# One visit instead of two for the scan outputs of blocks four to six, fewer and wider dummies at the start, and new planner settings

## The chip, the core and the metric

The kernel runs on one core of a Trainium2 chip, alone. The metric is device time of one execution in microseconds (us). A core has five engines with a queue of instructions each: PE (TensorE, the matmuls, with PEld for its weight loads), DVE (VectorE), ACT (ScalarE), POOL (GpSimd) and SP (SyncE, which here issues nearly all DMAs). [...]

## The reference, cut to what matters

A decaying linear attention runs over 768 positions in chunks; its output `y` is the input of a gated feed-forward network. There are 4 batches, 8 heads, head size 32 and state size 16; the network is 256 wide with 1536 hidden units.

```python
L = np.exp(cum[:, :, :, None] - cum[:, :, None, :]) * causal      # decays inside a chunk
M = np.einsum('bhin,bhjn->bhij', Cc, Bc) * L                      # scores
y_intra = np.einsum('bhij,bhjd->bhid', M, xc)
y_inter = np.einsum('bhin,bhnd->bhid', Cc, state) * decay_to_i[:, :, :, None]
y[:, :, sl] = y_intra + y_inter
state = decay_full[:, :, None, None] * state + np.sum(Bx, axis=2)
...
g, val = x @ w_gate, x @ w_val            # x: y of all heads side by side
return (g * (1.0 / (1.0 + np.exp(-g))) * val) @ w_out
```

## The kernel before, in words

The positions are cut into six blocks of 128 (`k` = 0 to 5 in the code, blocks one to six in the text), and each block into two pieces of 64. For each block PE does two short stretches of small fp32 matmuls. The first, `sums` and `scores`, makes the state sums (tiles `st`) and the scores (tiles `S`) in one go. The second, `outputs`, makes `y`: for each batch `values` adds scores times `x` (tiles 64 rows by 32 columns of the array, reading `L` and `xb`), then `carried` adds the earlier state (32 by 64, reading `bc` and `T`). Each such matmul of the program runs as two passes on the chip, and each pass is two instructions, a weight load and a matmul. So `outputs` of two batches is 64 passes of `values` and 32 of `carried`, 192 instructions.

Between these stretches stands the network. A hidden group `f` (twelve of 128 units) has gate and value banks `gv`, and its part of the output product goes to the banks `po`. These are matmuls of 512 columns in fp32r, three for each product (high times high, low times high, high times low), two instructions each; only the first eight groups of block one use whole fp32 (tiles `xf`, two passes per matmul). Part of block four, and blocks five and six as a pair, use a scheme with seven products in place of eight on sums of quarters (tiles `hx`, `hy`, `hz`; `px`, `py`, `pz`, `pr`; in the closing product `ox`, `oy`, `oz`, `or`). The high and low parts of the weights are made on ACT and DVE (`w_high`, `w_low`), and the whole weights are written back to DRAM (tiles `uncut`) for the sums that the scheme needs.

The order on every engine comes from a planner. Each operation is given an engine, a cost, a due time (its rank), what it needs, and the buffers that it takes and gives back; the planner then plays the program through, choosing the earliest due of the operations that are ready. `LEAD` says how long before a block's first hidden group its scan work is due; `LATER`, `MAKE`, `MAKE_STEP`, `AHEAD`, `URGENT`, `OUT_MAKE`, `OUT_STEP`, `BEHIND`, `AFTER`, `EARLY`, `SUM_LAG` and `SCAN_ALL` set due times and order of the preparing work on ACT and DVE, of the fetches and of the closing product, and `LATE` says which weight load the block loads of block three wait behind. In blocks two to six the output passes are planned as two visits of two batches, with a pause between them that no engine spends:

```python
add("PE", 1.52, do(outputs, k, (0, 1)), z + 11, need, ..., gives=("y", k, 0), kind="f", ...)
add("~", 2.6, lambda: None, z, [("y", k, 0)], gives=("pause", k))
add("PE", 1.52, do(outputs, k, (2, 3)), z + 11, [("pause", k)], ..., gives=("y", k), kind="f")
```

All users of `y` (`x_high`, `x_low`, `half_keep`, `x_keep`) wait for the second visit. Before the first real matmuls PE runs dummies (tile `rest`, function `idle`), 28 of 100 columns each.

Of the kernel before, what the change touches and what calls it, by code (L numbers as in the profile page):

```python
# [17 lines left out]
BATCH, H, S, D, N = 4, 8, 768, 32, 16  # L18
# [10 lines left out]
NF = DFF // P  # L29
# [14 lines left out]
class Plan:  # L44
# [26 lines left out]
    def add(self, engine, cost, run, rank, needs=(), takes=(), uses=(), gives=None, kind=None, lag=0.0, rows=1.0, slack=0.0):  # L71
        engines = [(engine, cost)] if cost is not None else engine
        self.ops.append(Op(engines, run, rank, needs, takes, uses, gives, kind, lag, rows, slack))
# [139 lines left out]
def scan_moe_kernel(ctx: ExitStack, tc, rows, decays, bc, xb, wgv, wo, cst, out):  # L213
# [847 lines left out]
    def do(f, *a):  # L1061
        return lambda *e: f(*a, *e)
# [6 lines left out]
    add = plan.add  # L1069
# [30 lines left out]
    for n, ranks in enumerate(IDLE):  # L1100
        for i, r in enumerate(ranks):
            need = [("idle", n, i - 1)] if i else [("idle", n - 1, len(IDLE[n - 1]) - 1)] if n else []
            if n:
                need = need + [(("S", 0, BATCH - 1), ("vals", 0), ("y", 0))[n - 1]]
            takes = [] if i or n else [("at", "rest")]
# [32 lines left out]
    for k in range(NB):  # L1138
        r = due(k)
        SLACK = min(k / 2, 1.0)  # L1140
        z = -5 if not k else r + LEAD[k]
        L, E, BC, XB, CZ, TT = ("L", k), ("E", k), ("bc", k), ("xb", k), ("Cz", k), ("T", k)
# [16 lines left out]
        if not k:  # L1159
# [3 lines left out]
            for b in range(BATCH + 1):  # L1163
                for i in range(2 if b < BATCH else 1):
# [7 lines left out]
                    need = [t, ("decays", 0), "dj"] + ([("scan0", b - last_one)] if i else []) + ([("M", 0, NP - 2)] if b == BATCH else [])  # L1172
# [16 lines left out]
        y = [("y", k, i) for i in range(2 * K)]  # L1189
        for bs in [(b,) for b in range(BATCH)] if not k else [range(BATCH)]:  # L1190
# [4 lines left out]
            if k in JOINED:  # L1195
# [3 lines left out]
                need = [("bt", k, BATCH - 1), ("Cz", k)]  # L1199
# [11 lines left out]
        for q in range(0 if k else 1, len(st)):  # L1211
            need = [*before, ("E", k), ("ap", k, q)] + ([] if k or q > 1 else [("ap", k, 0), ("round", 2)])
            add("DVE", 0.785, do(step, k, q), z + (8 if k else 25) + q, need, uses=[] + ([("T", k - 1)] if k and not q else []), gives=("step", k, q))
            before = [("step", k, q)]
        uses = [L, E, XB, BC, *y, TT]
# [3 lines left out]
        for g in range(0 if k else 2):  # L1219
            need = [("M", 0, p) for p in (2 * g, 2 * g + 1)]  # L1220
            add("PE", 0.45, do(values, 0, range(BATCH), (g,)), -1.4 + 0.1 * g, need, takes=[("mm", y[2 * q + g]) for q in range(K)], uses=[L, XB, *y], gives=("vals", g), kind="f")
        if k:
            need = [*(("M", k, p) for p in range(NP)), ("ce", k), *steps]
            add("PE", 1.52, do(outputs, k, (0, 1)), z + 11, need, takes=[("at", i) for i in y], uses=y, gives=("y", k, 0), kind="f", slack=min(k - 0.5, 2.5))
            add("~", 2.6, lambda: None, z, [("y", k, 0)], gives=("pause", k))
            add("PE", 1.52, do(outputs, k, (2, 3)), z + 11, [("pause", k)], uses=[L, *uses], gives=("y", k), kind="f")
        for b in range(0 if k else BATCH):
            add("PE", 0.135, do(carried, 0, b), -1, [("vals", 0), ("vals", 1), ("ce", 0), *steps], uses=uses, gives=("y", 0) if b == BATCH - 1 else ("y", 0, b), kind="f")
        done = [("y", k)]
# [71 lines left out]
    for r in range(NF // 2):  # L1301
        at = OUT_MAKE + OUT_STEP * r
        i = NF + r
        u = [("sg", ("out", r, n)) for n in range(2)]
        add("DVE", 0.6, do(whole_again, r), at, [("wl", i), ("wh", i), ("round", NW - 1), MIXED_AFTER, *prior], takes=u, gives=("ws", i, -1))
        uses = [key for _, key in u]
# [6 lines left out]
    for k in (*HALVED, PAIR):  # L1313
        for f in user(k):
            other = in_raw(f) if k == PAIR else f in LOOSE.get(k, ())
            need = [("spared", f), *behind, *(["new_t1", "new_t2"] if other and k == PAIR else [("xtl", k, 1)] if other else [])]
# [20 lines left out]
    for f in range(NF):  # L1337
# [27 lines left out]
        for b in range(2):  # L1365
            home, need = stay_home(f // 2, f"{f % 2 + 1}{b + 1}")
# [3 lines left out]
    for r in range(R):  # L1370
        at = due(PAIR, 2 * r + 1) + SUM_LAG
        pr = [("pr", PAIR + b, 2 * r + o) for b in range(2) for o in range(2)]
        for n, (t, *_) in enumerate((("t1",), ("t3",), ("t2",), ("t4",))):
            home, need = stay_home(r, t) if t != "t3" else ([], [])
            add("DVE", 0.6, do(stay_sum, r, n), at + n * 0.1, [*(pr if not n else [("ksum", r, n - 1)]), *need], takes=home, gives=("ksum", r, n))

    at = due(PAIR) + 60.0
# [23 lines left out]
    for j, (n, r, h) in enumerate(steps):  # L1401
# [5 lines left out]
        uses = [tile_of[b]]  # L1407
# [109 lines left out]

CST = W + 2 + 2 * D + 2 * P
NA = NB * K * BATCH * H // P
WARM = 28, 100  # L1520
IDLE = [-9.0] * WARM[0], [-1.45] * 4, [-1.35] * 2, [1000.0] * 3
LATER = 2.4
ST_ONE, ST_MM, JOINED = (), (1, 2, 3, 4), (1, 2, 3, 4)
LEAD = {1: -27.4, 2: -41.8, 3: -59.2, 4: -69.7, 5: -56.2}
PAIR_LAG, MIXED, RAW = 5.0, 4, 4
MIXED_AFTER = ("y", 1)
HALVED = {3: 4}
HALF_AT = "z"
MAKE, MAKE_STEP = 114.1, 3.3
LOOSE = {3: (3, 5, 7)}  # L1530
AHEAD, URGENT = 13.9, 58.5


def in_raw(f):
    return f >= MIXED and f % 2 == 0


OUT_MAKE, OUT_STEP = 181.0, 1.4
OUT_RAW = 1, 3, 5
BEHIND, AFTER = 0.9, 0  # L1540
MORE = 3
EARLY, SUM_LAG = 7.7, 8.0
STAYS = "11", "12", "21", "22", "t1", "t2", "t4"
SPARE = ("L", 0), ("E", 0), ("bc", 0), ("xb", 0), ("Cz", 0), ("T", 0), ("T", 1), ("dj", 0), ("dn", 0), ("w", 0)
MADE = (
# [15 lines left out]
    return f >= HALVED.get(k, NF)  # L1561


SCAN_ALL = 18.0
WHOLE = 8
LATE = {2: NF + 2}
GATE, HASTE = dict(bc=0, aj=0, xb=0, an=1), 7
HELD = {1: ("M", 0, 0), 2: ("M", 0, 1), 3: ("M", 0, 3)}

# [51 lines left out]
```

## Time and profile before

| | |
|---|---|
| runs of the kernel before, us | 336.28, 338.09, 338.64 (median 338.09) |
| profiled execution, us | 336.26 |
| its span, first to last instruction, us | 334.5 |
| PE busy | 328.5 us, 98% |
| DVE busy | 290.1 us, 87% |
| ACT busy | 192.6 us, 58% |
| DMA moved | 57.68 MB, mean 172 GB/s |

The profiled execution is 1.76 us longer than its span. The chain is the view that follows the last instruction back to what released it. A timeline row gives the start, the time until its last instruction's end, the instruction with its tiles and shapes, how many of a kind stand in a row (x), and in brackets how long the engine was idle before and who ended that; "issue" there means that the profile shows nothing that was waited for.

### The profile page before, as it was taken

Reading aid. Unit: us, or ns where it says so; the run is one execution under the profiler, and the core shown is the slowest. Engines: PE = TensorE matmul, PEld = TensorE weight load, DVE = VectorE, ACT = ScalarE, POOL = GpSimd, SP = SyncE. Lnnn points to the kernel's source line nnn. Section 1 sums busy time; section 2 is a strip of 40 time slices with the busy share of each in tenths; the row PEclk is TensorE's granted clock in tenths of the full one; section 3 lists DMA queues with packets and bytes.
Section 4 is the critical chain, followed back from the end, with each engine's and each line's share of the span. In section 5 each row is a group of like instructions: output and inputs, shape, how many; then the busy total and the mean of one; then the engine's idle time right before and its main releaser. Section 6 shows DMA issues by size and latency. Waiting matters only on the chain.

```text
span 334.5 us, 7903 instructions
## 1 busy us (share of the span) xinstructions
PE 328.5 (98%) x3196; PEld 259.6 (78%) x3199; DVE 290.1 (87%) x556; ACT 192.6 (58%) x360; POOL 4.2 (1%) x11
## 2 busy tenths in 40 slices
PE   8899999999999999999999999999999999999995
PEld 7634567888887888888888889998788888888784
DVE  5999999977988996998999955986768999989994
ACT  3686998365564663444464445543755556554982
POOL 1300000000000000000000000000000000000000
PEclk9999999999999999999999999999999999999999
DMA  6699569992011996466994399442047511330011
GB/s 246 223 306 335 209 201 341 292 211 75 17 33 38 248 375 212 175 222 213 270 386 174 125 315 186 136 151 105 2 126 252 189 58 72 123 125 0 3 64 63
DMA packets 21277, 57.68 MB, mean 172 GB/s; under 512 B 2296, under 2 KB 3320, under 8 KB 21240
## 3 DMA queue, kind: packets, MB, share of 16 engines
q1 hardware_dynamic: 20808, 56.94, 53.5%
q8 instruction: 25, 0.41, 0.5%
q10 hardware_dynamic: 432, 0.23, 0.2%
q14 instruction: 12, 0.10, 0.1%
HBM read 41.23 MB, written 15.93 MB: 171 GB/s over the span
## 4 chain that ended last, share of the span: by engine, by line
PE 97%; DMA 1%; issue 1%; DVE 0%; ACT 0%; DVEq 0%
PE gv L202 35%; PE po L202 20%; PE py L202 7%; PE y L202 5%; PE px L202 5%; PE oy L202 4%; PE hy L202 3%; PE pz L202 2%; PE pr L202 2%; PE ox L202 2%; PE S L202 2%; PE hz L202 2%; PE hx L202 2%; PE a L202 2%; PE st L202 1%; PE or L202 1%
## 5 line engine op out<-in xcount | busy, mean ns | idle before, releaser
L202 ACT CAST hh<-sg 128x512 fp32r<-128x512 f32 (+1 forms) x54 | 29.3, 556 | 32.2 <-PE po L202 24.5
L202 DVE TENSOR_TENSOR hl<-sg,hh 128x512 fp32r<-128x512 f32 (+1 forms) x56 | 32.8, 608 | 8.6 <-ACT hh L202 8.3
L202 ACT ACTIVATE sg<-gv 128x512 f32<-128x512 f32 x40 | 23.9, 599 | 26.8 <-PE gv L202 24.7
L202 DVE TENSOR_TENSOR sg<-gv,sg 128x512 f32<-128x512 f32 x40 | 27.2, 684 | 4.5 <-PE gv L202 4.5
L202 DVE TENSOR_TENSOR_SCAN L<-L,dj 128x520 f32<-128x520 f32 x20 | 24.1, 1228 | 0.0
L202 DVE TENSOR_TENSOR ws<-ws 128x128 f32<-128x128 f32 (+1 forms) x60 | 20.0, 364 | 1.9 <-ACT ws L202 1.6
L202 DVE TENSOR_TENSOR L<-S,L 128x512 f32<-128x512 f32 x24 | 15.6, 683 | 3.5 <-PE S L202 3.5
L202 ACT ACTIVATE sg<-px 128x512 f32<-128x512 f32 x12 | 7.2, 599 | 15.9 <-PE px L202 15.9
L202 PE MATMUL py<-xht,ws 128*128 128x512 f32 x48 | 15.3, 400 | 0.0
L202 DVE TENSOR_TENSOR hlt<-stt,hht 128x512 fp32r<-128x512 f32 x18 | 11.7, 686 | 0.9 <-ACT hht L202 0.7
L202 PEld LDWEIGHTS y<-L,xb 64*32 64x32 f32 x768 | 8.5, 105 | 4.5 <-issue 4.1
L202 ACT ACTIVATE sg<-pz 128x512 f32<-128x512 f32 x12 | 7.2, 599 | 7.2 <-PE pz L202 7.2
L202 PE MATMUL y<-L,xb 64*32 64x64 f32 x768 | 10.6, 224 | 0.4 <-issue 0.4
L202 ACT CAST ws<-ws 128x512 fp32r<-128x512 f32 x10 | 6.2, 622 | 8.2 <-DVE ws L202 6.7
L202 ACT ACTIVATE Cz<-bc,cs 128x512 f32<-128x512 f32 x12 | 8.0, 716 | 4.7 <-DMA bc<-in_bc 4.7
L202 PEld LDWEIGHTS py<-xht,ws 128*128 128x128 f32 x48 | 8.6, 188 | 2.7 <-DVE pz L202 1.2
L202 DVE TENSOR_TENSOR ps<-py,ps 128x512 f32<-128x512 f32 x12 | 8.3, 689 | 2.6 <-PE py L202 2.6
L202 ACT CAST hht<-stt 128x512 fp32r<-128x512 f32 x17 | 9.8, 620 | 0.7 <-DVE stt L202 0.6
L202 DVE TENSOR_TENSOR pz<-py,ps 128x512 f32<-128x512 f32 x12 | 8.3, 695 | 1.3 <-PE py L202 1.0
L202 PE MATMUL py<-xlt,ws 128*128 128x512 f32 x24 | 9.3, 389 | 0.0
L202 PE MATMUL y<-bc,T 32*64 32x64 f32 x352 | 7.6, 223 | 0.2 <-issue 0.2
L202 ACT COPY py<-px 128x512 f32<-128x512 f32 x12 | 6.9, 574 | 1.3
(792 smaller groups left out, 974.2 us busy)
## 6 DMA issues: line engine op xcount, KB each, us to landing
ws<-keep SPq DMA_DIRECT2D x20, 512.0 KB, 4.3
keep<-ws SPq DMA_DIRECT2D x12, 512.0 KB, 7.3
L<-clipped SPq DMA_DIRECT2D x10, 520.0 KB, 9.3
xb<-in_xb SPq DMA_DIRECT2D x6, 768.0 KB, 10.3
bc<-in_bc SPq DMA_DIRECT2D x6, 512.0 KB, 8.9
ws<-uncut SPq DMA_DIRECT2D x12, 256.0 KB, 3.1
wos_k<-keep SPq DMA_DIRECT2D x6, 512.0 KB, 3.6
out<-ob SPq DMA_DIRECT2D x8, 256.0 KB, 4.1
```

Source lines behind the costliest of these rows:

```text
L202: ins = getattr(self.engine, name)(*a, **k)
```

## The change: what it does

For blocks four to six (`MERGED = 3, 4, 5`) the two visits become one: `outputs` of all four batches, first 128 passes of `values`, then 64 of `carried`, 192 passes or 384 instructions; the pause goes. Blocks two and three keep two visits. The dummies become 11 of 256 columns. Fourteen further settings of the planner get other numbers.

```diff
         if k:
             need = [*(("M", k, p) for p in range(NP)), ("ce", k), *steps]
-            add("PE", 1.52, do(outputs, k, (0, 1)), z + 11, need, takes=[("at", i) for i in y], uses=y, gives=("y", k, 0), kind="f", slack=min(k - 0.5, 2.5))
-            add("~", 2.6, lambda: None, z, [("y", k, 0)], gives=("pause", k))
-            add("PE", 1.52, do(outputs, k, (2, 3)), z + 11, [("pause", k)], uses=[L, *uses], gives=("y", k), kind="f")
+            takes = [("at", i) for i in y]
+            if k in MERGED:
+                add("PE", 2.64, do(outputs, k, range(BATCH)), z + 11, need, takes=takes, uses=[L, *uses], gives=("y", k), kind="f", slack=min(k - 0.5, 2.5))
+            else:
...
-WARM = 28, 100
+WARM = 11, 256
...
-LATER = 2.4
+LATER = 3.3
...
-LEAD = {1: -27.4, 2: -41.8, 3: -59.2, 4: -69.7, 5: -56.2}
+LEAD = {1: -31.9, 2: -52.2, 3: -70.6, 4: -74.9, 5: -46.5}
...
-MAKE, MAKE_STEP = 114.1, 3.3
+MAKE, MAKE_STEP = 122.9, 4.8
...
-AHEAD, URGENT = 13.9, 58.5
+AHEAD, URGENT = 9.0, 41.6
...
-OUT_MAKE, OUT_STEP = 181.0, 1.4
+OUT_MAKE, OUT_STEP = 174.5, 2.3
...
-BEHIND, AFTER = 0.9, 0
+BEHIND, AFTER = 0.7, 2
...
-EARLY, SUM_LAG = 7.7, 8.0
+EARLY, SUM_LAG = 0.3, 11.7
...
-SCAN_ALL = 18.0
+SCAN_ALL = 21.3
+MERGED = 3, 4, 5
...
-LATE = {2: NF + 2}
+LATE = {2: NF}
```

On PE, block four's outputs before, the first visit's end, what stands between, and the second visit's beginning (`y` are the four output banks, `xb`, `L`, `bc` and `T` the block's inputs; the rows left out are more passes of the same kinds):

```order
L202 MATMUL y_3_1941<-bc_1512,T_1489 64x64
L202 MATMUL gv_5_1_1999<-xh_920,wg5h 128x512 x2
L202 MATMUL gv_5_1_1999<-xh_920,wg5l 128x512 x2
L202 MATMUL gv_5_1_1999<-xl_921,wg5h 128x512 x2
L202 MATMUL gv_6_0_2009<-xh_920,wg6h 128x512 x2
...
L202 MATMUL gv_6_1_2020<-xl_921,wg6h 128x512 x2
L202 MATMUL y_0_1938<-L_1487,xb_1485 32x64
```

On PE, the same block's outputs now, with what stands ahead, at the seam of `values` and `carried`, and behind:

```order
L202 MATMUL po_1_0_1557<-hh_11_1734,wo5l 128x512
L202 MATMUL gv_0_1_1791<-xh_914,wg0h 128x512 x2
L202 MATMUL gv_0_1_1791<-xh_914,wg0l 128x512 x2
L202 MATMUL gv_0_1_1791<-xl_915,wg0h 128x512 x2
L202 MATMUL y_0_1804<-L_1448,xb_1446 32x64
...
L202 MATMUL y_3_1807<-L_1448,xb_1446 32x64
L202 MATMUL y_0_1804<-bc_1472,T_850 64x64
...
L202 MATMUL y_3_1807<-bc_1472,T_1450 64x64
L202 MATMUL gv_1_0_1918<-xh_914,wg1h 128x512 x2
```

The 18 matmuls of 512 columns that separated the visits have gone elsewhere. Before, the visits stood within hidden group five and behind group six of block three's network; the one visit now stands behind its group zero.

On SP, the DMA issues from the load `wo0r` on, before (`uncut` is a write of 256 KB, `wo..r` a load of 512 KB):

```order
L202 DMA wo0r<-in_wo 128x1024
L202 DMA uncut<-wg8w 128x512
L202 DMA uncut<-wg0w 128x512
L202 DMA uncut<-wg1w 128x512
L202 DMA uncut<-wg9w 128x512
L202 DMA wo1r<-in_wo 128x1024
L202 DMA uncut<-wg2w 128x512
L202 DMA uncut<-wg3w 128x512
L202 DMA uncut<-wg4w 128x512
```

On SP, the same place now:

```order
L202 DMA wo0r<-in_wo 128x1024
L202 DMA uncut<-wg8w 128x512
L202 DMA uncut<-wg0w 128x512
L202 DMA uncut<-wg1w 128x512
L202 DMA uncut<-wg2w 128x512
L202 DMA uncut<-wg3w 128x512
L202 DMA uncut<-wg4w 128x512
L202 DMA uncut<-wg5w 128x512
L202 DMA wo1r<-in_wo 128x1024
L202 DMA uncut<-wg9w 128x512
```

Seven writes now stand ahead of the load `wo1r`, where there were four, and the write of group nine stands behind it.

The change moves everything on PE against a grid of 256 instructions. Counted in the built programs from 0 (an fp32 matmul is four instructions, an fp32r one two, a wait that stands alone one), PE has 6456 instructions before and 6418 now, and the counts 192 + 256 j lie here:

| count | before | now |
|---|---|---|
| 448 | instruction 84 of block one's first `values` | instruction 118 of the same |
| 704 | first matmul of group zero's second bank (`gv`, whole fp32) | first matmul of group two's second bank |
| 1216 | 101 of block two's first output visit | 136 of it |
| 1472 | 126 of block two's second visit | 175 of it |
| 2752 | in a `po` stretch | 28 of block four's `st` and `S` |
| 3008 | 83 of the `S` part of block four | in `po`, 27 behind block four's `S` |
| 3264 | 76 of block four's first visit | 221 of its only visit |
| 3520 | 103 of block four's second visit | in `gv` |
| 4288 | 149 of block five's first visit | 205 of its only visit |
| 5312 | 98 of block six's first visit | 177 of its only visit |

Between block two's two visits stood 18 matmuls of 512 columns (group nine and half of ten); now there are 12 (group nine).

## Rows read from the trace of the kernel before

**Rows 1.** The page: busy time of the engines, instruction queue, chain that ended last.
```profile
PE 328.5 (98%) x3196; PEld 259.6 (78%) x3199; DVE 290.1 (87%) x556; ACT 192.6 (58%) x360; POOL 4.2 (1%) x11
...
q8 instruction: 25, 0.41, 0.5%
...
PE 97%; DMA 1%; issue 1%; DVE 0%; ACT 0%; DVEq 0%
```

**Rows 2.** Waits of PE in the whole span: total us, times, longest.
```profile
PE gv L202 <- PE gv L202: 0.6, 1, 0.6
PE y L202 <- issue: 0.6, 2, 0.4
```

**Rows 3.** Timeline of PE at block 4's two output visits: start, us, instruction.
```profile
147.53 0.62 PE L202 MATMUL gv<-xh,wg5l 128*128 128x512 f32 x2
147.98 0.61 PE L202 MATMUL gv<-xl,wg5h 128*128 128x512 f32 x2
148.53 0.86 PE L202 MATMUL y<-L,xb 64*32 64x64 f32 x64
149.32 0.69 PE L202 MATMUL y<-bc,T 32*64 32x64 f32 x32
149.94 0.72 PE L202 MATMUL gv<-xh,wg5h 128*128 128x512 f32 x2
150.50 0.63 PE L202 MATMUL gv<-xh,wg5l 128*128 128x512 f32 x2
...
154.26 0.86 PE L202 MATMUL y<-L,xb 64*32 64x64 f32 x64
```

**Rows 4.** The page, two groups (decay scans, output passes): count, busy us, mean ns.
```profile
L202 DVE TENSOR_TENSOR_SCAN L<-L,dj 128x520 f32<-128x520 f32 x20 | 24.1, 1228 | 0.0
...
L202 PE MATMUL y<-L,xb 64*32 64x64 f32 x768 | 10.6, 224 | 0.4 <-issue 0.4
```

**Rows 5.** Timeline of PE, start of the program.
```profile
0.82 2.49 PE L202 MATMUL rest<-const-bfloat16-1.0 128*128 128x100 bf16 x28 [0.82 <-PEq L1610]
3.43 4.88 PE L202 MATMUL a<-rows 128*128 128x260 f32 x16
...
12.67 0.42 PE L202 MATMUL y<-L,xb 64*32 64x64 f32 x21 [0.39 <-issue]
...
18.23 1.88 PE L202 MATMUL gv<-xf,wg0w 128*128 128x512 f32 x4 [0.61 <-PE gv L202]
19.94 3.60 PE L202 MATMUL gv<-xf,wg1w 128*128 128x512 f32 x8
```

**Rows 6.** Windows from 0: PE and PEld instructions begun (x) up to three waits.
```profile
0.00:12.40 12.40, 11.19 (x220) 8.75 (x221) 9.01 (x19) 4.73 (x9) 4.19 (x11) 1.00 0.61 209
0.00:18.10 18.10, 15.82 (x344) 11.46 (x348) 14.35 (x31) 8.78 (x17) 4.19 (x11) 1.00 0.72 247
0.00:55.60 55.60, 53.14 (x722) 31.74 (x725) 51.30 (x102) 42.77 (x80) 4.19 (x11) 1.00 0.80 264
```

**Rows 7.** Timeline of PE, the two output visits of block 2.
```profile
48.95 0.86 PE L202 MATMUL y<-L,xb 64*32 64x64 f32 x64
...
54.69 0.86 PE L202 MATMUL y<-L,xb 64*32 64x64 f32 x64
55.72 0.69 PE L202 MATMUL y<-bc,T 32*64 32x64 f32 x32 [0.17 <-issue]
```

**Rows 8.** Windows: last three columns are PEclk, DMA share, GB/s.
```profile
12.00:16.00 4.00, 3.29 (x148) 2.26 (x136) 3.64 (x9) 3.35 (x10) 0.00 (x0) 1.00 0.90 298
...
130.00:134.00 4.00, 4.00 (x138) 3.15 (x137) 0.91 (x3) 2.31 (x6) 0.00 (x0) 1.00 0.44 119
```

**Rows 9.** Timeline of PE, a visit of state sums and scores (block 4).
```profile
131.40 0.86 PE L202 MATMUL st<-xb 64*32 64x64 f32 x64
...
133.33 0.72 PE L202 MATMUL gv<-xh,wg0h 128*128 128x512 f32 x2
```

**Rows 10.** Timeline of DVE: the rounding that frees the second weight group.
```profile
18.58 0.68 DVE L202 CUSTOM_DVE_ANT_0 wg1w<-wg1r,wg1w 128x1024 uint16<-128x1024 uint16 x1
```

More of the change, by code (lines that the diff above doesn't have):

```diff
@@ L1223, in scan_moe_kernel @@
             need = [*(("M", k, p) for p in range(NP)), ("ce", k), *steps]
-            add("PE", 1.52, do(outputs, k, (0, 1)), z + 11, need, takes=[("at", i) for i in y], uses=y, gives=("y", k, 0), kind="f", slack=min(k - 0.5, 2.5))
-            add("~", 2.6, lambda: None, z, [("y", k, 0)], gives=("pause", k))
-            add("PE", 1.52, do(outputs, k, (2, 3)), z + 11, [("pause", k)], uses=[L, *uses], gives=("y", k), kind="f")
+            takes = [("at", i) for i in y]
+            if k in MERGED:
+                add("PE", 2.64, do(outputs, k, range(BATCH)), z + 11, need, takes=takes, uses=[L, *uses], gives=("y", k), kind="f", slack=min(k - 0.5, 2.5))
+            else:
+                add("PE", 1.52, do(outputs, k, (0, 1)), z + 11, need, takes=takes, uses=y, gives=("y", k, 0), kind="f", slack=min(k - 0.5, 2.5))
+                add("~", 2.6, lambda: None, z, [("y", k, 0)], gives=("pause", k))
+                add("PE", 1.52, do(outputs, k, (2, 3)), z + 11, [("pause", k)], uses=[L, *uses], gives=("y", k), kind="f")
         for b in range(0 if k else BATCH):
```

## The prediction

> **What bounds the kernel now.** I read the page first, then the waits of PE, then its timeline. On the page PE is busy 98% of the span and holds 97% of the chain that ended last; DVE, the next engine, is busy 87% [rows 1]. So the end moves only by what PE does, and by what keeps PE from doing it. The list of PE's waits has little in it: its largest entry is 0.6 us, one wait of a `gv` matmul for nothing but the `gv` matmul ahead of it, and the next are two of the output passes for "issue", 0.6 us together [rows 2]. The timeline then shows two more kinds of loss inside "busy": the cost of going into and out of the small passes, and gaps with no partner. Three gaps matter. The output passes of block one stop for 0.39 us before 12.67, group zero's second bank stops for 0.61 us before 18.23 [rows 5], and in block two's second visit the `carried` passes begin at 55.72 after 0.17 us of nothing, although all they wait for has run [rows 7].
>
> What do these three have in common? By the windows PE and PEld had begun 441, 692 and 1447 instructions by then [rows 6]. With the 7, 12 and 25 instructions that only wait, which the windows don't count, these are 448, 704 and 1472, that is 192 + 256 times 1, 2 and 5. No other stop of PE of this size lies elsewhere in the main part. The instruction queue moved 25 packets, 0.41 MB [rows 1], 16.4 KB each, one for every 258 of PE's 6456 instructions. I take it that a block of 256 instructions is asked for when PE passes one such count, and that PE stops at the next count when the block has not come.
>
> How long does the block take? From the count at 448, resumed at 12.67, to the one at 704, resumed at 18.23, it is 5.6 us, with the DMA engines busy 0.9 of the time in that stretch [rows 5, 8]. For block two, count 1216 lies 50 passes into the first visit. A pass takes (0.86 - 0.22) / 63 = 0.0102 us, from the group's 64 passes and the mean of one, 224 ns [rows 4, 7]. So the count is at 48.95 + 0.51 = 49.46, and PE went on at 55.72: 6.2 us [rows 7]. Where block four's two visits carry counts 3264 and 3520, at 148.53 + 0.39 and 154.26 + 0.53, 5.9 us were enough [rows 3].
>
> [...]
>
> **Merging the visits.** At block four a pair of network matmuls starts 0.45 us after the pair ahead (147.53 to 147.98). Going in: 147.98 to 148.53 is 0.55, so 0.10 more. The 64 passes of `values` take 148.53 to 149.32, 0.79; at 0.0102 each they need 0.65, so 0.14 goes into the change to the other tile shape. The 32 passes of `carried` take until 149.94, 0.62; (0.69 - 0.22) / 31 = 0.0152 each gives 0.49, and 0.13 goes into the way back. The first pair behind takes 150.50 - 149.94 = 0.56, 0.11 more [rows 3, 4]. A visit is 0.10 + 0.79 + 0.62 + 0.11 = 1.62 us, of which 0.48 is fixed. Two visits cost 3.24, one of double length 0.48 + 2 x 1.14 = 2.76. That saves 0.48 for each of three blocks, **1.44 us**, all on PE and so on the path. The ends: 0.21 each if the two inner parts (0.14 and 0.13) grow with the passes, 0.63 us in all, and 1.65 us if the short bubbles within the passes are shared too.
>
> The users of `y` waited for the second visit and wait now for the only one, so nobody gets it later within a visit, and the four output banks are held for 2.8 us where it was from 148.53 to over 155 [rows 3]. During the visit PE hands nothing to ACT; ACT is busy 58% [rows 1], so it catches up. The 18 matmuls that stood between the visits are run elsewhere at the same price.
>
> **Where the counts fall now.** Each merged visit has 384 instructions, so one count always falls into it and two can, 256 instructions or about 1.5 us apart, far below what a block took above. Here only one falls into each. For block four the sum to it, from the count before: 2752 lies 14 passes into the state sums, the rest of that visit is 133.33 - 131.40 - 0.15 = 1.78 [rows 9], then 13 and a half matmuls at 0.227 = 3.06, with 0.11 to get going: 4.95 us to count 3008. From there 11 `po` and 6 `gv` matmuls, 3.85, 0.10 to go in and 110 passes, 1.12: 5.1 us to 3264. For blocks five and six the same sum gives about 7. So block four is inside what a block of instructions has taken at its slowest (5.6 and 6.2), and outside what a quiet DMA should need; the DMA share at its place was 0.44 [rows 8]. I take no stop there; the bounds are 0 and 6.2 - 4.95 + 6.2 - 5.1 = 2.35 us.
>
> Block two gets tighter. From 1216 to 1472: 28 passes of `carried` 0.43 and 0.13 out, 12 matmuls 2.72 with 0.11 lost behind and 0.10 ahead, `values` 0.79, 23 passes 0.36: 4.65 us where 6.2 were taken. If the block takes as long, PE stops 1.55 us, against 0.24 now (55.72 less 54.69 + 0.79). But seven weight write-backs now go out before the load `wo1r`, and fewer stand in the queue with it, so the block should come sooner. Bounds: -0.24 and +1.3; I take **+0.4**, the nearer to the lower end because the traffic moved ahead.
>
> **The start.** The dummies are 28 x 100 = 2800 columns before, 11 x 256 = 2816 now. 28 took 2.49 us, and `a` begins at 3.43 when its rows are in [rows 5]: no change. With 34 instructions fewer ahead, count 704 moves from group zero to group two, some 7 us later (3.4 us per group), and by then 12 us have passed since 448: the 0.61 us stop goes. What is late next is group one, which needs its rounding on DVE, done at 18.58 + 0.68 = 19.26; PE would want it at 19.94 - 0.61 = 19.33 [rows 5, 10]. So **-0.6 us**, bounds -0.75 (with the slow restart behind the stop) and 0. The stop at 448 stays; it has as many instructions since count 192 as before, with 34 dummies' instructions gone from ahead of it: 0, bounds -0.4 and +0.3. [...]
>
> **The other settings.** They move work on DVE, ACT and SP, not its amount. Cover is that PE is never waiting for DVE in the main part [rows 2] with DVE 13% free; if it is gone at a place, a scan or two of 1.2 us [rows 4] is the price (third rival). Cost 0.
>
> **Sum.** -1.44 + 0.4 - 0.6 = -1.64 us against the profiled execution: 336.26 - 1.64 = 334.6. That execution was the fastest seen, with 336.28; the median is 338.09. The four times' mean is 337.27. From the mean the forecast would be 335.6, from the median 336.45; I say **336.0 us**, halfway, 0.6% under the median.
>
> **Rivals.** First, the instruction blocks come too late: all of 1472, 3008 and 3264 at 6.2 us each. Then 1.3 + 1.25 + 1.1 = 3.65 is lost against 2.04 gained: 337.9 by the profiled execution, 339.7 by the median, slower than before. It decides from a block time of about 5.7 us on at block four. For it, two of the rows above; against it, the quiet DMA there. Chance 0.1. Second, the stop at 704 is not the counts' doing and stays, and so may 55.72's: -1.44 alone, 334.8 and 336.65. Against it stands that three stops agree in a number of 256. Chance 0.12. Third, the new order makes PE wait for DVE, at the scans of block four or five, which now must be ready some 12 us earlier in PE's work: one scan's 1.2 us at two places gives 334.6 + 2.4 = 337.0, 338.4 by the halfway reading. Chance 0.1. Fourth, blocks take longer in most executions than in the profiled one, which was a fast one; then the stop at 704, directly behind the one at 448, costs 1.5 to 2 us in the others and its removal is worth that: 334.5 by the median reading. Chance 0.15. My forecast: 0.53.
>
> **Numbers.** The range holds the forecast with its bounds, the second and fourth rival and the third's time, and leaves out the first: 334.0 to 338.3. A measurement of this kernel can't tell under about 1% from no change, since its runs spread over 0.7%. Faster by over 1% means under 334.7: the fourth rival's better half and the low end of mine, 0.17. Slower by over 1%, over 341.5: 0.03, the first rival with worse block times. Within 1%: 0.80.
>
> **What would show it.** In the changed kernel's timeline a merged visit should take 2.75 to 2.8 us from the start of its first pass to 0.1 us into the work behind, with no gap in its `carried` or last `values` passes at the counts; gaps there speak for the first rival. Groups zero to two should run without a stop. Block two's second visit should show a gap of 0 to 1.5 us within `carried`, and the list of waits no new line of PE for DVE. The prediction is wrong if the merged visits cost over 3.2 us, or if PE has new waits of over 1 us in sum.

## The result, and the profile after

| | before | after |
|---|---|---|
| median, us (14 runs each, side by side) | 336.17 | 338.75 |
| lowest and highest, us | 335.25, 339.86 | 336.08, 341.78 |
| profiled execution and its span, us | 336.26, 334.5 | 340.26, 338.5 |

The ratio is 1.0060, 95% interval 1.0036 to 1.0084: slower by 0.6%. Here and below the times are medians of all executions, while a ratio leaves out those over 1.5% above the fastest of their kernel, three of the changed kernel's 14; by the medians of all it is 1.0077. The forecast was 336.0 us, and within 1% with a chance of 0.80. 338.75 lies just outside its range.

The page of the changed kernel (busy engines, granted clock in 40 slices, instruction queue) and the list of PE's waits:

```profile
PE 330.8 (98%) x3179; PEld 260.4 (77%) x3182; DVE 290.5 (86%) x556; ACT 192.7 (57%) x360; POOL 4.2 (1%) x11
...
PEclk9999969999999999999999999999999999999999
...
q8 instruction: 25, 0.41, 0.5%
```

```profile
PE S L202 <- issue: 2.2, 1, 2.2
...
PE y L202 <- issue: 0.2, 1, 0.2
```

PE is 2.3 us longer busy, the clock row has a 6 in its seventh slice, and there is a wait that the kernel before doesn't have: 2.2 us in `S`, for "issue". The entry of 0.6 us in `gv` is gone [rows 2]. Timeline of PE of the changed kernel, at block two's state sums and scores:

```profile
33.59 3.60 PE L202 MATMUL gv<-xf,wg5w 128*128 128x512 f32 x8
37.32 0.85 PE L202 MATMUL st<-xb 64*32 64x64 f32 x64
38.10 0.86 PE L202 MATMUL S<-Cz,bc 32*64 32x128 f32 x35
41.17 1.15 PE L202 MATMUL S<-Cz,bc 32*64 32x128 f32 x29 [2.21 <-issue]
42.25 6.33 PE L202 MATMUL gv<-xf,wg6w 128*128 128x512 f32 x8
48.42 3.60 PE L202 MATMUL gv<-xf,wg7w 128*128 128x512 f32 x8
...
59.07 0.86 PE L202 MATMUL y<-L,xb 64*32 64x64 f32 x64
59.86 0.95 PE L202 MATMUL y<-bc,T 32*64 32x64 f32 x32
```

The `S` passes stop behind the 35th. In the built program count 960, 256 behind 704, lies 34 passes into block two's `S`: the place agrees within one pass. What PE waits for there I take to be a block of instructions, since the profile names no engine and a packet of the instruction queue q8 ends shortly ahead. The DMA view of 38.3 to 38.4 us (queue, packets, MB, share of the 16 engines) has that packet:

```profile
q8 instruction: 1, 0.02, 93.3%
```

It takes 0.933 x 16 x 0.1 = 1.49 us and so lands at 39.8; PE goes on 1.37 us later. The traces of all runs of this case have 36 stops of PE of over 0.2 us behind the start-up for which the profile names no other engine, and in each PE goes on 1.2 to 1.6 us behind the end of a q8 packet.

After the stop everything is slow: 29 passes of `S` take 1.15 us, and the eight of group six 6.33 us, where group seven's eight take 3.60. Windows of the changed kernel (begin, end and length, then the busy us of PE, PEld, DVE, ACT and POOL; the last three columns are PEclk, DMA share, GB/s):

```profile
40.00:42.00 2.00, 0.83 (x29) 0.75 (x29) 0.90 (x2) 2.00 (x7) 0.00 (x0) 0.69 0.00 0
42.00:44.00 2.00, 2.00 (x15) 0.84 (x3) 1.65 (x3) 1.10 (x2) 0.00 (x0) 0.50 0.03 8
...
46.00:48.00 2.00, 2.00 (x5) 0.73 (x4) 0.00 (x0) 1.93 (x4) 0.00 (x0) 0.61 0.79 158
48.00:50.00 2.00, 2.00 (x6) 0.94 (x5) 1.31 (x3) 1.35 (x3) 0.00 (x0) 1.00 1.00 372
```

TensorE was granted half its clock (0.50 in the window from 42 us) for (1 - 0.69) / 0.5 x 2 = 1.2 us of the first window and 1.6 us of that from 46 on, so from about 40.8 to 47.6 us. It fell in the last 0.4 us of the stop, with nothing but `st` and `S` passes run since 37.32. That is not in every execution: by the list of runs, the mean clock of 7 of the 14 was 0.995 or less, of the other 7 0.999 or more, and those have a median of 337.44, still 1.3 us over the kernel before. Of the kernel before, 6 of the 136 executions beside the experiments below had a clock that low.

The start and block four of the changed kernel, which answer to [rows 5] and [rows 3]:

```profile
3.55 5.25 PE L202 MATMUL a<-rows 128*128 128x260 f32 x16 [0.23 <-DVE rows L202]
...
13.17 0.30 PE L202 MATMUL y<-L,xb 64*32 64x64 f32 x4 [0.24 <-issue]
...
16.05 3.67 PE L202 MATMUL gv<-xf,wg0w 128*128 128x512 f32 x8
19.79 3.67 PE L202 MATMUL gv<-xf,wg1w 128*128 128x512 f32 x8
```

```profile
140.99 0.62 PE L202 MATMUL gv<-xh,wg0l 128*128 128x512 f32 x2
141.44 0.61 PE L202 MATMUL gv<-xl,wg0h 128*128 128x512 f32 x2
141.99 1.49 PE L202 MATMUL y<-L,xb 64*32 64x64 f32 x128
143.40 1.16 PE L202 MATMUL y<-bc,T 32*64 32x64 f32 x64
144.49 0.73 PE L202 MATMUL gv<-xh,wg1h 128*128 128x512 f32 x2
145.07 0.62 PE L202 MATMUL gv<-xh,wg1l 128*128 128x512 f32 x2
```

Group zero runs its eight passes in one go, from 16.05. Group one starts at 19.79, only 0.15 us sooner than before (19.94, [rows 5]): `a` took 5.25 us in place of 4.88 this time (and 4.35 in the run `e2` below, with the same dummies). Of its 16 passes the first seven took 551 to 771 ns each, where before the first five took 604 to 771; the others took 382 to 390 ns in both. The merged visit has no stop: 141.99 - 141.44 - 0.45 = 0.10 to go in, 1.41 of `values`, 1.09 of `carried`, 145.07 - 144.49 - 0.45 = 0.13 to come out, 2.73 us in sum.

The balance of the two profiled executions: +2.21 for the stop, + 6.33 - 3.60 = 2.73 and 1.15 - 0.69 = 0.46 for the half clock (29 passes take 0.69 us at full clock in the run `h1` below), -0.15 at the start, 3 x (2.73 - 3.24) = -1.53 for the merges, +0.1 for a wider gap in block two's second visit (`carried` in 0.95 us for 0.69, where it was 0.17 of idle [rows 7]). That is 3.8 of the 4.0 us.

### The profile page after: what moved, and what is told of

Read it like the earlier page. It is cut to its first block, busy times and chain, and to the rows that moved or that the text cites. A ratio compares the mean times of both kernels' runs of the same rounds, so it can differ in the third digit from the quotient of the medians.

```text
span 338.5 us, 7866 instructions
## 1 busy us (share of the span) xinstructions
PE 330.8 (98%) x3179; PEld 260.4 (77%) x3182; DVE 290.5 (86%) x556; ACT 192.7 (57%) x360; POOL 4.2 (1%) x11
## 4 chain that ended last, share of the span: by engine, by line
PE 97%; issue 1%; DMA 1%; DVE 1%; ACT 0%; DVEq 0%
PE gv L202 35%; PE po L202 20%; PE py L202 7%; PE px L202 5%; PE y L202 5%; PE oy L202 3%; PE hy L202 3%; PE pz L202 2%; PE pr L202 2%; PE ox L202 2%; PE S L202 2%; PE a L202 2%; PE hz L202 2%; PE hx L202 2%; PE st L202 1%; PE oz L202 1%
## 5 line engine op out<-in xcount | busy, mean ns | idle before, releaser
L202 ACT CAST hht<-stt 128x512 fp32r<-128x512 f32 x18 | 10.6, 621 | 1.4 <-PE or L202 1.3
L202 PE MATMUL S<-Cz,bc 32*64 32x128 f32 x384 | 8.0, 290 | 2.2 <-issue 2.2
L202 PE MATMUL y<-L,xb 64*32 64x64 f32 x768 | 9.9, 225 | 0.2 <-issue 0.2
L202 PEld LDWEIGHTS S<-Cz,bc 32*64 32x64 f32 x384 | 6.2, 136 | 3.3 <-issue 2.4
```

What stands on the lines that cost most here:

```text
L202: ins = getattr(self.engine, name)(*a, **k)
```

## The experiments

My theory after the result: the block of instructions needed at 960 is asked for at 704, which the new dummies moved 7 us later, and then waits among the data DMAs; the stop lowers the clock; the merges gain what was forecast. The rivals: the merged visits cost the time; the new order of block two's scan work costs it by itself. All ratios are to the kernel before, run beside. "Half clock" counts the executions with a mean granted clock of 0.996 or less.

### One part undone, one part alone

**Old dummies in the changed kernel** (`e1`).
```diff
-WARM = 11, 256
+WARM = 28, 100
```


> The changed kernel with the old dummies, 28 of 100 columns, which puts 34 instructions back ahead of everything, so that count 704 lies in group zero again and count 960 at instruction 34 of block two's S part. Theory (the block of instructions needed at 960 is asked for at 704 and waits among the data DMAs; after the stop the granted clock halves): asked for 7 us earlier, the block is there; no stop at 960, no half clock near 40 us, a stop of about 0.6 us at 704 comes back. About 338.7 - 5.8 + 0.6 = 333.5 to 334.8, or 0.993 to 0.997 of the kernel before. Rival (the new order of the scan work at block two, or the merged visits, cost the time): the stop or the loss stays, 338 to 339, 1.006.


336.64 us, 1.0009 (0.9981 to 1.0037); half clock in 2 of 12. The stop at 960 is gone, and that at 704 is back with 2.26 us, not 0.6:

```profile
20.27 1.88 PE L202 MATMUL gv<-xf,wg0w 128*128 128x512 f32 x4 [2.26 <-issue]
...
40.03 1.21 PE L202 MATMUL S<-Cz,bc 32*64 32x128 f32 x64
```

So in the new order the dummies' instructions decide whether PE stops at 960, but putting them back gains about 2 us only, by the medians. Expected were 4 to 5.

**New dummies in the kernel before** (`e2`).
```diff
-WARM = 28, 100
+WARM = 11, 256
```


> The kernel before with the new dummies alone, 11 of 256 columns: 34 instructions fewer, count 704 in group two, count 960 at instruction 59 of block two's S part, which still stands within group six. Theory: the block asked for 7 us later comes too late, a stop of 1 to 2.5 us at 960, and the half clock behind it if the stop is what lowers the clock; the 0.6 us at 704 go: 336.2 + 0.5 to 5 = 336.7 to 341, most likely 339.5 (1.010). Rival (the order or the merged visits): no stop, 0.6 us gained, 335.6 (0.998).


336.67 us, 1.0013 (0.9989 to 1.0038), half clock in none of 12, and no stop at 960. My theory missed: count 704 lies in group two here too. The dummies alone don't make the stop. Nor do they gain: the forecast 0.6 us would be a ratio of 0.998, which lies below the interval.

**No merge in the changed kernel** (`e3`).
```diff
-MERGED = 3, 4, 5
+MERGED = ()
```


> The changed kernel with two visits in all blocks (no block merged), all else as changed. The order up to block three's end is the changed kernel's, so the stop at 960 and the half clock stay in every theory. Theory (a merge saves 0.48 us per block): 338.7 + 1.4 = 340.2, 1.010 to 1.012 of the kernel before. Rival (the merged visits are what costs): 336 to 337, 1.000.


340.13 us, 1.0111 (1.0070 to 1.0151), half clock in 4 of 8, a stop of 1.66 us in `S`. Slower than with the merges by 1.3 us by the medians (1.0116 against 1.0077); the intervals of the two ratios overlap. The rival, 1.000 without the merges, is out: they are not what costs.

**The merge alone in the kernel before** (`e4`).
```diff
+            if k in MERGED:
+                add("PE", 2.64, do(outputs, k, range(BATCH)), ...)
+            else:
...
+MERGED = 3, 4, 5
```


> The kernel before with the merge of blocks four to six alone, all settings and dummies as before. Counts 448 to 2752 lie as before; 3264 and 3520 both fall into block four's visit, 256 instructions and about 1.7 us apart. Theory: no stop at 960, the merge saves 1.44 us: 334.8, 0.996; if two counts so close make PE stop at 3520, that costs up to 4 us of block time, then 336 to 338. Rival (the merged visits cost): 337.5 or more, 1.004, without a stop at any count.


337.01 us, 1.0018 (0.9996 to 1.0039), half clock in 2 of 12. In the profiled execution the gain was eaten by a stop in block four's visit, into which counts 3264 and 3520 both fall (PE also waits 0.74 us for DVE before 216.25):

```profile
148.13 1.49 PE L202 MATMUL y<-L,xb 64*32 64x64 f32 x128
149.55 0.81 PE L202 MATMUL y<-bc,T 32*64 32x64 f32 x38
151.77 0.40 PE L202 MATMUL y<-bc,T 32*64 32x64 f32 x13 [1.42 <-issue]
```

3264 lies 38 passes in, at 148.13 + 0.39 = 148.52; PE went on at 151.77. From the count to there it was 3.25 us, with a DMA share of 0.06 from 148 to 150 us; the stop between, 1.42 us, is what two counts cost in this visit.

**The kernel before, blocks five and six merged, 22 dummies** (`b22`).
```diff
-WARM = 28, 100
+WARM = 22, 127
...
+MERGED = 4, 5
```


> The kernel before with 22 dummies of 127 columns and only blocks five and six merged (block four keeps two visits, so that no two counts fall into one visit). Theory: 0.48 for each merge, 0.6 to 2 for the stop at 704, against no stop elsewhere: 336.2 - 0.96 - 0.6 = 334.6, 0.9955. Rival (merging gains nothing): 335.6 to 336.2.


336.38 us, 1.0015 (0.9983 to 1.0046), half clock in 4 of 12. In the profiled execution PE stops for 1.35 us before 233.36 in block six's visit: 5568 falls into it besides 5312, which I had not counted.

### Where the count lies

**22 dummies in the changed kernel** (`c22`).
```diff
-WARM = 11, 256
+WARM = 22, 127
```


> The changed kernel with 22 dummies of 127 columns: nothing moves on any engine but the counts, by 22 instructions against the changed kernel. 704 lies at group one's beginning, near 20 us, some 7 us behind 448 and 3 us sooner than now; 960 at instruction 46 of S, 1472 at 153. Theory: late enough for the block asked for at 448 and early enough for the one needed at 960: no stop at 704 (under 0.5), none at 960; 448 and 1472 lose 0.3 to 0.8 each as ever, 3008 up to 0.9: 334.5 to 335.5, 0.996. Rival (the loss is in the new order): 338 or more.


336.93 us, 1.0038 (1.0004 to 1.0072), half clock in 5 of 12. In the profiled execution PE stopped for 2.09 us at 960 all the same, though 704 lies 3 us earlier. Against my theory.

**Block two's scan work due as before** (`l1`), the changed kernel otherwise.
```diff
-LEAD = {1: -31.9, ...
+LEAD = {1: -27.4, ...
```


> The changed kernel with block two's scan work due as before (LEAD of block two back to -27.4): its st and S passes stand in the middle of group six again, 2 us of matmuls later, and 18 matmuls stand between its two output visits; the dummies stay new, so 704 stays in group two and 960 comes at instruction 59 of S. Theory (the block asked for at 704 lands near 38 us whenever it is asked for, with the end of the loads, so what decides is when PE reaches 960): no stop at 960, no half clock, no gap at 1472, a stop of about 0.6 us behind 5312, since 5568 now falls into block six's visit too: 334.5 to 335.3, 0.9965. Rival (asking late at 704 is the whole of it): stop at 960 stays, 337 to 339.


334.93 us, 0.9981 (0.9959 to 1.0002), half clock in none of 12, no stop at 960 beyond 0.26 us (the 64 passes of `S` take 1.47 us, 1.21 in `e1`), nor the 0.6 us that I expected behind 5312 (the visit ends 12 instructions ahead of 5568):

```profile
36.36 1.88 PE L202 MATMUL gv<-xf,wg6w 128*128 128x512 f32 x4
38.17 0.86 PE L202 MATMUL st<-xb 64*32 64x64 f32 x64
38.96 1.47 PE L202 MATMUL S<-Cz,bc 32*64 32x128 f32 x64
40.35 1.98 PE L202 MATMUL gv<-xf,wg6w 128*128 128x512 f32 x4
```

The block needed at 960 moved earlier. Its packet, in the DMA view of 36.6 to 36.8 us, begins 1.5 us ahead of the first `st` pass; in the changed kernel it began 1.0 us behind it:

```profile
q8 instruction: 1, 0.02, 40.6%
```

This one number undone gives back 1.0060 - 0.9981 = 0.8%, some 2.6 us. (It also puts 18 matmuls back between block two's two output visits; what the stop at 1472 takes, 0.1 to 0.8 us, is part of that.) The `st` and `S` passes stand between the halves of group six here, as before the change; in the changed kernel they stand ahead of it. With the old dummies (`e1`) the new place does no harm, with the new dummies (`e2`, `l1`) the old place does none; together they make the stop.

**Places chosen, and the same with two visits** (`v13`, `v13_two_visits`).
```diff
-WARM = 11, 256
-LEAD = {1: -31.9, 2: -52.2, 3: -70.6, 4: -74.9, 5: -46.5}
+WARM = 13, 216
+LEAD = {1: -27.4, 2: -52.2, 3: -70.6, 4: -74.9, 5: -50.0}
```


> As the run with block two's old place, with 13 dummies of 216 columns and block six's scan work due 3.5 us earlier (LEAD -50), chosen so that by the count no stretch of 256 instructions is short: 5.8 us at 1216, 5.1 at 2240, 3.7 at 2752, all others over 5.6, and no visit holds two counts. Theory: no stops but 448's 0.3 to 0.6: 334.0 to 334.8, 0.995. Rival (the three merges don't give what the places take): 336, 1.000.


335.05 us, 0.9991 (0.9972 to 1.0009), 0.3 us over what I expected.
```diff
-MERGED = 3, 4, 5
+MERGED = ()
```


> As the run with the places chosen, but with two visits in every block (none merged). Up to block four's outputs it is the same program, and no stretch of 256 instructions behind is short. The difference of the two is the merge alone: theory 1.44 us (bounds 0.63 and 1.65), so 335.5 to 336.2, 0.999 to 1.000. Rival (merging is worth nothing, or costs): the same time as the merged one or less.


336.40 us, 1.0011 (0.9988 to 1.0034). Half clock in none of 12 of either. The three merges are worth 336.40 - 335.05 = 1.35 us where nothing stops at 960; by the means of the 12 executions of each it is 1.2, give or take 0.6.

**The same with the old dummies** (`v28`).
```diff
-WARM = 13, 216
+WARM = 28, 100
```


> The version with the places chosen (three merges, block two's old place) with the old dummies, 28 of 100 columns: 704 goes back into group zero, 4.3 us of passes behind 448, 960 to instruction 25 of S; no visit holds two counts. Theory (what the new dummies take away at 704 is a real gain): a stop of 0.6 to 2.3 us at 704 comes back, 335.05 + 0.6 to 2.3 = 335.7 to 337.4, 1.000 to 1.004 of the kernel before. Rival (the dummies' 34 instructions are worth nothing beside the execution's own spread): 335.0, 0.998.


335.38 us, 0.9967 (0.9929 to 1.0006), half clock in 2 of 12; in the profiled execution nothing stops at 704. The rival was nearer: no loss from the old dummies shows beside the 0.9991 of `v13`.

### What the block waits for

**Loads of groups nine to eleven held until group four is done** (`h1`), in the changed kernel, and **of ten and eleven until group five is done** (`h2`).
```diff
-HELD = {1: ("M", 0, 0), 2: ("M", 0, 1), 3: ("M", 0, 3)}
+HELD = {..., 9: ("gv", 0, 4, 1), 10: ("gv", 0, 4, 1), 11: ("gv", 0, 4, 1)}
```


> The changed kernel, dummies and counts as changed, but the loads of weight groups nine to eleven (0.5 MB each, now issued at 25 to 30 us) wait for group four's last matmul, near 33 us. Count 960 stays at instruction 68 of block two's S part, asked for at the same 704. Theory (the block waits for its turn among the data DMAs): with 1.5 MB less queued it comes some 4 us sooner; no stop at 960, no half clock behind it: 338.7 - 3 to 5.8 = 333 to 335.7, if the later loads make nobody wait. Rival (the stop hangs on the place of the count in the passes alone, whatever the DMAs do): the 1.7 to 2.5 us stop stays, 338 to 339.


338.71 us, 1.0076 (1.0044 to 1.0109), half clock in 7 of 12, stop 0.94 us.
```diff
+HELD = {..., 10: ("gv", 0, 5, 1), 11: ("gv", 0, 5, 1)}
```


> As the run with held loads, but only groups ten and eleven wait, for group five's last matmul near 36 us; order and counts are the changed kernel's up to one instruction. Theory: the queue is empty some 2.5 us sooner than before, the stop of 1.7 to 2.5 us shrinks to under 0.5 or goes: 334 to 336.5. Rival (place alone): stop stays, 338 to 339.


341.93 us, 1.0102 (1.0034 to 1.0170), half clock in 4 of 6, stop 1.76 us. Neither tells much: in `h1` the planner put the closing weights' loads into the free place, and the DMA share stayed at 0.97 and above until 36 us.

**The closing weights' loads held too** (`h3`), until group five is done.
```diff
+HELD = {..., 9: ("gv", 0, 4, 1), ..., 12: ("gv", 0, 5, 1), ..., 17: ("gv", 0, 5, 1)}
```


> The changed kernel, counts as changed (704 in group two, 960 at instruction 68 of S, ahead of group six), but the loads of groups nine to eleven wait for group four's last matmul near 33 us, and the closing weights' loads for group five's; in the first such run the closing weights' loads had taken the free place, so the DMA engines stayed full. 18 matmuls stand between block two's two output visits here. Theory (the block waits among the data DMAs): the engines run empty some 4 us sooner, the block comes by 33 us, no stop at 960, no half clock: 334 to 335.5. Rival (the place of the count in the passes alone): stop of 1 to 2.5 us stays, 337.5 to 339.


340.76 us, 1.0140 (1.0099 to 1.0182), half clock in 5 of 6, stop 2.58 us. The DMA share was 0.67 and 0.60 from 32 to 36 us, then the held loads came (1.01 from 36 to 38 us). The stop was no shorter.

**All of them held until group six's first bank, behind `S`** (`h4`).
```diff
+HELD = {..., 9: ("gv", 0, 6, 0), ..., 17: ("gv", 0, 6, 0)}
```


> The changed kernel with the loads of groups nine to eleven and of the closing weights held until group six's first bank, which stands behind block two's st and S: nothing is loaded between 22 us and then but what was issued before, so the DMA engines run empty near 33 us. Count 960 stays at instruction 68 of S ahead of group six, asked for at the same 704. Theory (the block comes when the loads issued by then have drained, and not before): it lands near 34 us; no stop at 960, no half clock; groups nine to eleven may wait 0 to 3 us for their late weights: 334.5 to 338, clock 0.998 or more in nearly all runs. Rival (the block takes its 12 to 18 us from the request, or comes at this place whatever the DMAs do): stop of 1.5 to 2.6 us and half clocks stay, 338.5 to 342.


335.90 us, 0.9990 (0.9958 to 1.0023), half clock in 1 of 12. The stop is 0.94 us; it didn't go, though the DMA share was 0.36 and 0.33 in 32 to 36 us. It fell between the two theories: 0.9990 in place of 1.0060, but by the DMA view no packet of q8 moved between 34 and 36.5 us.

**The load E held too** (`h5`), **then group eight's** (`h6`).
```diff
...
+        if k == 1:
+            wait_for(ins, ("gv", 0, 6, 0))
...
```


> As the run with the loads held behind S, and the load E of block two (260 KB of 2080 byte pieces, there issued at 32 us, the last traffic ahead of the block) waits with them. Between 21 us and the end of the S passes nothing is asked of the DMA engines, which were empty of the earlier loads near 33 us. Theory (the block comes when the traffic ahead of it has drained): it lands 3 us sooner, no stop at 960 at all. Rival (something else than traffic holds it until group five ends): the same stop of 0.9 us or more. The total is no measure here: groups nine to eleven get their weights late, and counts 1216 and 1472 stand 3.2 us apart: 335.5 to 340.


342.02 us, 1.0174 (1.0125 to 1.0223), half clock in 4 of 4, stop 1.35 us.
```diff
+HELD = {..., 8: ("gv", 0, 6, 0), 9: ("gv", 0, 6, 0), ...
```


> As the run with E held too, and the load of group eight waits with them as well, so that the last load ahead is issued near 19 us and the engines are empty near 31 us. Theory (traffic): no stop at 960, and no half clock in any run. Rival (not traffic): the stop of 0.9 us or more stays at the same place. Group eight's weights come late, so PE waits for them 2 to 5 us behind group seven: 337 to 342 in either case; what decides is the stop.


343.63 us, 1.0231 (1.0173 to 1.0288), half clock in 4 of 4, stop 1.93 us. Of `h6` the windows (last three columns as above), the timeline of PE, and the DMA view of 37.2 to 40 us:

```profile
32.00:34.00 2.00, 2.00 (x6) 0.88 (x5) 2.00 (x2) 0.92 (x2) 0.00 (x0) 1.00 0.06 25
34.00:36.00 2.00, 2.00 (x6) 0.76 (x4) 2.00 (x4) 1.49 (x3) 0.00 (x0) 1.00 0.02 4
36.00:38.00 2.00, 1.11 (x65) 0.72 (x64) 2.00 (x4) 0.91 (x2) 0.00 (x0) 1.00 0.00 0
...
42.00:44.00 2.00, 2.00 (x4) 0.94 (x3) 2.00 (x5) 0.00 (x0) 0.00 (x0) 0.50 0.03 8
```

```profile
37.28 0.85 PE L202 MATMUL st<-xb 64*32 64x64 f32 x64 [0.89 <-ACT sg L202]
38.06 0.86 PE L202 MATMUL S<-Cz,bc 32*64 32x128 f32 x35
40.85 0.69 PE L202 MATMUL S<-Cz,bc 32*64 32x128 f32 x29 [1.93 <-issue]
```

```profile
DMA packets 1, 0.02 MB, mean 6 GB/s; under 512 B 0, under 2 KB 0, under 8 KB 0
...
q8 instruction: 1, 0.02, 2.6%
```

The DMA engines do next to nothing from 34 us on, and still PE stops at 960. The one packet that moves between 37.2 and 40 us is of queue q8; between 30 and 37.2 us none of q8 moved. So traffic didn't hold it here: the packet began 1.03 us behind the first `st` pass. My theory fell here. (PE later waits 3.5 us for group eight's weights; that is what makes the total long.)

**A new theory: asked for at instruction 768** (`h7`), 64 behind 704. In the nine kernels until then that don't stop at 960 the packet had moved about when PE was there, at instructions 765 to 781. `h6` with 18 instructions more ahead:
```diff
-WARM = 11, 256
+WARM = 20, 140
```


> As the run with E and group eight held too, where the DMA engines stand idle from 34 us on and the stop stayed, but with 20 dummies of 140 columns, 18 instructions more ahead: instruction 768 (64 behind 704) lies 14 instructions ahead of the st passes, in group five's second bank, where it was the st passes' fifth; count 960 lies at instruction 50 of S in place of 68. New theory (the block needed at 960 is asked for when PE comes to 768, not to 704, and takes some 1 us with idle DMA engines, then 1.3 us to the first instruction): asked for 3 us before the st passes, it is there in time: no stop at 960, none of the half clock near 41 us. Rival (something holds the block until the st passes begin, wherever 768 lies): a stop of 1.5 to 2.5 us at 960 as before. PE still waits 3 us or so for group eight's late weights; total 339 to 342.


345.31 us, 1.0251 (1.0195 to 1.0306), half clock in 4 of 4, stop 2.35 us. The timeline of PE and the DMA view of 39.1 to 42 us:

```profile
33.10 3.60 PE L202 MATMUL gv<-xf,wg5w 128*128 128x512 f32 x8
39.19 0.85 PE L202 MATMUL st<-xb 64*32 64x64 f32 x64 [2.49 <-ACT sg L202]
...
42.99 1.55 PE L202 MATMUL S<-Cz,bc 32*64 32x128 f32 x38 [2.35 <-issue]
44.47 5.68 PE L202 MATMUL gv<-xf,wg6w 128*128 128x512 f32 x8
```

```profile
DMA packets 1, 0.02 MB, mean 6 GB/s; under 512 B 0, under 2 KB 0, under 8 KB 0
...
q8 instruction: 1, 0.02, 2.0%
```

768 was in group five's second bank, run by 36.7 us; the engines were all but idle (0.09 MB from 33 to 39.1 us) and PE itself waited for 2.49 us in front of `st`; yet the packet moved behind 39.1 us. This theory fell too, and its rival held in these two runs: the packet began behind the first `st` pass, by 1.03 us in `h6` and by 1.45 us in `h7`.

**17 dummies with the places chosen** (`v17`).
```diff
-WARM = 13, 216
+WARM = 17, 165
```


> The version with the places chosen with 17 dummies of 165 columns: instruction 768 lies 17 instructions ahead of st, in group five, and 704 in group one. New theory: asked for near 33 us, the block is there with more to spare than with 13 dummies (asked for near 36 us), and 704 comes late enough for its own block: no stop at 704 or 960 in any run, 334.5 to 335.2, 0.996 to 0.998. Rival (the spread has other causes): the same 335.05 and the same spread as with 13.


335.12 us, 0.9953 (0.9927 to 0.9980), half clock in none of 12, 334.28 to 336.19. Faster than the kernel before by some 0.5%; but by its own median it is the same as with 13 dummies, and the kernel before ran at 336.68 beside it, where it was 335.79 beside those. The timeline, and the DMA view of 36.8 to 39.3 us:

```profile
36.83 1.88 PE L202 MATMUL gv<-xf,wg6w 128*128 128x512 f32 x4
39.40 0.86 PE L202 MATMUL st<-xb 64*32 64x64 f32 x64 [0.69 <-DVE xb L202]
40.19 0.67 PE L202 MATMUL S<-Cz,bc 32*64 32x128 f32 x24
41.13 0.91 PE L202 MATMUL S<-Cz,bc 32*64 32x128 f32 x40 [0.28 <-issue]
```

```profile
q8 instruction: 1, 0.02, 2.7%
```

Here the packet moved ahead of the first `st` pass. Counted from 0, `st` begins at instruction 785 here and at 782 in `h7`, three apart, and the packet came on different sides of it. In the changed kernel `st` is at 764, and the packet began 1.0 us behind its first pass. Nor does a border between 782 and 785 fit all runs: in `c22` `st` begins at 786, and the packet still began 0.96 us behind its first pass. (DMA was busy there, with a share of 1.01 from 34 to 36.2 us and 0.81 in the next.) What asks for a block is not shown.

What the twenty traces do show is a clean split by the packet for 960. In the ten that stop there for 0.9 us or more (the changed kernel, `e3`, `c22` and `h1` to `h7`) it began 0.3 to 2.1 us behind the first `st` pass. In the ten others it began 1.0 to 6.0 us ahead of it.

## Why the prediction was wrong

**The other settings, cost 0**: this step failed. I said that they move work on DVE, ACT and SP. `LEAD` of block two moved work on PE, its `st` and `S` passes, from the middle of group six to its front. `l1`, that number alone undone, has no stop of over 0.26 us at 960 and no half clock in 12 executions, 0.9981 in place of 1.0060. The prediction's own sign of being wrong came with it: new waits of PE of over 1 us in sum, 2.21.

**The start, -0.6**: the mechanism was right and incomplete. 704 moved to group two and its stop went, but the next block came later too, and count 960 was neither in my table nor in the sum. The packet for 960 began at 32.96 us in the kernel before, at 35.97 with the new dummies alone (`e2`), and at 38.30 in the changed kernel. What I took off, 0.61 us, came back there as 2.21 us, and the half clock, seen in half of the executions, cost 3.2 us more in the profiled one. It needed both: with the old dummies (`e1`) or the old place (`e2`, `l1`) PE doesn't stop at 960. As a gain the dummies were mis-sized too: `e2`, with the new ones alone, is no faster than the kernel before, `v28`, with the old ones, is no slower than `v13`, and the stop that they take away was 0.6 us in one execution, 2.26 in another (`e1`) and nothing in two more (`e4`, `v28`). No run shows the slow restart that the bound of -0.75 counts: in the kernel before, the four passes behind that stop took 589 to 592 ns each, and those of group one behind them 592.

**The bounds: a block is asked for when PE passes one count.** The counts themselves held: every stop for "issue" of over 0.3 us named above stands at one. That the block is asked for at the count ahead was not shown: in `h6` no packet of q8 moved from 30 to 37.2 us, in `h7` none from 33 to 39.1 us, both behind 704 and with the engines all but idle from 34 us on. With it fell the block times of 5.6 and 6.2 us: with idle engines PE went on 3.0 us (`h5`), 3.6 (`h6`) and 3.8 (`h7`) behind the first `st` pass, and 3.25 us behind the count in `e4`.

**The merges, -1.44**: right; 1.35 us between two kernels without a stop at 960, and 2.73 us a visit where 2.76 was forecast. **Where the counts fall, 0 for block four**: right, no stop at 3008 or 3264. That only one count may fall into a visit was said in passing and carries more than I thought: two cost 1.42 us (`e4`) and 1.35 us (`b22`). **Block two, +0.4**: 0.1 us in the profiled execution, 0.7 to 0.8 in `e1` and `e3`.

**The base.** The forecast started from three executions with a median of 338.09; the 14 beside the changed kernel have 336.17. So the miss is larger than 338.75 against 336.0 looks: 1.64 us were to be gained, and 2.6 were lost. Two slips of the working change little: 49.46 to 55.72 is 6.26 us, not 6.2, and the four times' mean is 337.32, not 337.27.

Of the rivals, the first (blocks come too late) named the kind of stop that came, at the wrong places; at 3008 and 3264 nothing stopped in the changed kernel. The second, that 704 is not the counts' doing, has `e1` against it, where the stop comes back with 34 instructions of dummies. The third, waits of PE for DVE, didn't come: the changed kernel has none of over 0.25 us. The fourth took the profiled execution, 336.26, for a fast one, and it is not: the median of 14 is 336.17.

## What to carry to other kernels

Where an engine is busy 98% of the time, list every count at which it can stop for instructions (here 192 + 256 j, at which every such stop of over 0.3 us named above stands), for the whole program, before costing an edit that adds or removes instructions, and look at how fast PE comes to each through stretches of many short passes (`st`, `S`, `outputs`). Here PE came from the first `st` pass to 960 in 38.96 - 37.32 = 1.64 us, where with idle DMA engines it went on 3.0 to 3.8 us behind that pass (`h5` to `h7`). Count a planner's due times as edits of the order on the bound engine until the order says otherwise. And look at how many executions have a low clock, not only at one profile: here it was 7 of 14 against 6 of 136.

## What the runs showed of the hardware

- PE went on 1.2 to 1.6 us behind the end of a packet of the instruction queue, in all 36 stops of over 0.2 us for which the profile names no other engine.
- A packet of the instruction queue came late with a DMA share of 0.02 and 0.00 in the 4 us from 34 to 38 us (`h6`); it began only behind the first `st` pass, by 1.03 us, and by 1.45 us where PE had waited 2.49 us in front of that pass (`h7`). Which instruction asks for a block stays open.
- In the profiled executions the granted clock fell to half for 6.8 us behind stops of 2.21 (changed kernel), 2.35 (`h7`) and 2.58 us (`h3`) between the passes of `S`, and for 3.4 us behind 1.93 us where PE had waited 0.89 us ahead of `st` too (`h6`); not behind 0.94, 1.35, 1.66 and 1.76 us, nor behind 2.09 us in `c22`, nor behind 2.26 us at 704, between matmuls of 512 columns (`e1`). It fell for 3.4 us behind waits for late weights of 1.82 (`h5`), 3.49 (`h6`) and 3.53 us (`h7`) too. So the length of the stop alone does not tell which are followed by the half clock.
